# A decode-attention kernel: short instruction streams by loops, chunks of 64 keys, both output weights loaded last

## The chip, the cores and the metric

One core of one Trainium2 chip runs the whole program. The metric is device time in microseconds (us) of one execution. Unless a number is said to come from a profile it is the median of the timed runs; a profiled execution gives a span, which is some 2 us shorter than the time.

## The reference

Two independent attention blocks, A and B, each with its own weights and its own cache; the outputs are put side by side.

```python
B, Sq, D = 8, 1, 1024            # eight sequences, one new token each
H, Sk, Dh = 32, 4096, 128        # heads, cached keys, head size; all bf16
q = (x @ wq).reshape(B, Sq, H, Dh).transpose(0, 2, 1, 3)
scores = einsum("bhqd,bhkd->bhqk", q, k_cache) * Dh ** -0.5
o = einsum("bhqk,bhkd->bhqd", softmax(scores), v_cache)
out = o.transpose(0, 2, 1, 3).reshape(B, Sq, H * Dh) @ wo
```

Nothing of the caches is used twice. K and V of both blocks are 1073.7 MB, the four weights 33.6 MB, and all of it has to come from memory once.

## The kernel before

A tile is eight heads of one sequence: 128 partitions, each with 256 keys of 128 numbers, 64 KB a partition, 8.39 MB. There are 64 tiles of K and 64 of V. Three ring slots of that size hold what is loaded: two for K in turn, one for V.

VectorE multiplies a K tile by q chunk by chunk and folds it once; TensorE adds up the rest with identity matmuls; VectorE finishes the sum. After the whole tile: maximum, exponential (ACT), a masked copy `PM` of the probabilities (VectorE), and `PV` (TensorE), one tile behind.

```python
    CT = 32                                   # keys in a chunk
    NR = T // CT                              # 8 chunks a tile
    ...
        def make_mul(s):                      # VectorE, in place in the ring
            opMul[s] = add("dve", lambda e: e.tensor_tensor(
                v, v, qbc[:, n % 2, :].unsqueeze(1).to_broadcast([128, CT, Dh]), ALU.mult), [opT[("k", n, r)], opQbc[n]])
        def make_fold(s):                     # VectorE: 128 numbers to 64
        def make_eacc(s, fold):               # TensorE: 64 to 16, four identity matmuls a chunk
        def make_red(s):                      # VectorE: 16 to 1, two chunks later
    ...
        pv_at = {(n + 1, 5): n for n in range(NQ - 1)}   # PV after chunks 5 and 6 (counted from 0) of the next tile
```

The order of loads, and who frees a slot (cut):

```python
        put("wq", 0, 1); put("k", 0); put("wq", 1, 2)
        for n in range(NQ - 1):
            early = ...                                    # a K tile in two halves around wo
            put("k", n + 1, cuts=((0, NR // 2), (NR // 2, NR)) if early else None)
            put("v", n, 2)
            for c in range(NC):
                if n == done_at(c, NC, HB, B) + 1:         # n = 32 and n = 56
                    put("wo", c)                           # takes a K slot in the middle of the stream
                    late[n + 2] = c
        put("v", NQ - 1, cuts=...)                         # the last V in pieces
        put("wo_last", 0, 2)                               # the last 8 heads of B's wo
        plan.append(("v", NQ - 1, ((3 * NR // 4, 7 * NR // 8), (7 * NR // 8, NR))))
    ...
                    # B's wo: head h, row p to partition p: pieces of 2 KB
                    opT[(kind, n)] = dma(to[:, 0:cols].rearrange("p (h n) -> p h n", n=D),
                                         caches[-1][4][heads.start * Dh:heads.stop * Dh, :].rearrange("(h p) n -> p h n", p=128), key, [dep])
```

Everything is issued from straight lines of code: each engine's 64 tiles are written out, with every wait a constant.

## Time and profile before

| before | |
|---|---|
| time, median of 3 (range) | 2583.62 us (2583.49 to 2583.98) |
| profiled span | 2580.7 us |
| DMA | 1107.3 MB, 430 GB/s in the mean |
| VectorE busy | 2221.8 us, 86% |
| TensorE busy | 1219.7 us, 47% |
| one K and one V tile | 38.90 us |

From the page of the kernel before. `DMA` is the busy share in tenths in 40 equal slices, `GB/s` what moved in each; then the DMA queues with packets, MB and share of the time of all 16 DMA engines; then three groups of instructions (busy us, mean ns of one, and the idle time before them with its cause):

```profile
DMA  9999999999999999999999999999999999999998
GB/s 422 437 426 435 435 431 431 436 429 435 433 430 435 434 430 426 435 435 433 428 430 427 435 430 434 436 426 435 434 430 428 432 436 428 429 411 434 427 429 369
...
q1 hardware_dynamic: 23920, 1107.32, 99.5%
q8 instruction: 60, 0.98, 0.2%
q14 instruction: 18, 0.15, 0.0%
...
L305 DVE TENSOR_TENSOR ring<-ring,qbc 128x4096 bf16<-128x4096 bf16 x512 | 1169.0, 2283 | 327.0 <-DMA ring<-in_A_k_cache_dram 164.3
...
L310 DVE TENSOR_TENSOR ring<-ring 128x2048 bf16<-128x2048 bf16 x512 | 618.2, 1207 | 0.1
...
L327 DVE TENSOR_REDUCE s_sb<-red 128x32 f32<-128x512 f32 x512 | 348.3, 680 | 1.4 <-PE red L319 1.4
```

The DMA engines are busy throughout. VectorE idles before its multiply, 327 us in all, and what ends that idle time is a landing of K. Queue q1 holds the kernel's own loads. q8 and q14 hold instructions that the engines fetch: 78 packets, 1.13 MB, 0.2% of the time.

The timeline, one period of the steady state (start, duration, engine, line, operation; in brackets the idle time before it and its cause):

```profile
1015.35 2.29 DVE L305 TENSOR_TENSOR ring<-ring,qbc 128x4096 bf16<-128x4096 bf16 x1 [3.95 <-DMA ring<-in_A_k_cache_dram]
...
1046.41 0.33 SPq L158 DMA_DIRECT2D ring<-in_A_v_cache_dram  x1
...
1052.04 0.33 SPq L158 DMA_DIRECT2D ring<-in_A_k_cache_dram  x1
...
1054.25 2.29 DVE L305 TENSOR_TENSOR ring<-ring,qbc 128x4096 bf16<-128x4096 bf16 x1 [4.18 <-DMA ring<-in_A_k_cache_dram]
```

K lands at 1015.35 and at 1054.25: 38.90 us for 16.78 MB. The V load is issued 31.06 us into the tile, when PV has read the slot.

The chain of work that ended last, at the end of the kernel (start, duration, what):

```profile
2560.59 14.06 DMA ring<-in_B_v_cache_dram
...
2574.70 0.65 PE pv L359 x8
...
2575.37 0.61 ACT accS L367
...
2576.02 0.28 PE o L384 x4
...
2576.39 0.45 DVE on_sb L420
...
2576.88 1.08 PE proj L439 x32
...
2577.98 0.42 DVE orow L447
```

After the last piece of V lands at 2574.7, six short steps and the output follow, 6.0 us to the end of the span.

At the start, the second load of V and the load of K issued after it:

```profile
112.20 0.33 SPq L158 DMA_DIRECT2D ring<-in_A_v_cache_dram  x1
118.00 0.33 SPq L158 DMA_DIRECT2D ring<-in_A_k_cache_dram  x1
```

And the 40 us around B's `wo` (in the order of the columns: PE, PEld, DVE, ACT and POOL busy with counts, the clock, the DMA share, GB/s):

```profile
2290.00:2330.00 40.00, 18.23 (x196) 7.19 (x196) 21.50 (x18) 0.88 (x2) 0.00 (x0) 0.67 0.97 387
```

### The profile page before, as it was taken

To read this page: it belongs to the slowest core of one execution; us is meant where nothing else is said; L and a number is where in the kernel's file an instruction comes from. 1 tells how busy PE (TensorE), PEld (TensorE's weight loads), DVE (VectorE), ACT (ScalarE), POOL (GpSimd) and SP (SyncE) were. 2 spreads that over 40 slices of the span, in tenths; PEclk is the share of its full clock that TensorE was granted. 3 is DMA by queue.
4 is the path that set the end of the run, shared out by engine and by line. 5 is a ranking of instruction groups with operands and counts; after the bars stand their busy time and mean duration, and the time that the engine had idled before them with its cause. 6 is when DMAs were issued, how large, how long until landed. Compare 5 with 4: busy or idle time off the path is not lost.

```text
span 2580.7 us, 17905 instructions
## 1 busy us (share of the span) xinstructions
PE 1219.7 (47%) x7768; PEld 374.6 (15%) x7768; DVE 2221.8 (86%) x1809; ACT 105.2 (4%) x273; POOL 5.7 (0%) x23
## 2 busy tenths in 40 slices
PE   2454454453554454454553445445345445453445
PEld 0111111111111111111111111111112111110112
DVE  3898898898898898898895889889889889887897
ACT  1100000000000000000000000000000000000000
POOL 0000000000000000000000000000000000000000
PEclk7665655655656655656655566565565565565656
DMA  9999999999999999999999999999999999999998
GB/s 422 437 426 435 435 431 431 436 429 435 433 430 435 434 430 426 435 435 433 428 430 427 435 430 434 436 426 435 434 430 428 432 436 428 429 411 434 427 429 369
DMA packets 24094, 1108.50 MB, mean 430 GB/s; under 512 B 2304, under 2 KB 2368, under 8 KB 6480
## 3 DMA queue, kind: packets, MB, share of 16 engines
q1 hardware_dynamic: 23920, 1107.32, 99.5%
q8 instruction: 60, 0.98, 0.2%
q14 instruction: 18, 0.15, 0.0%
q10 hardware_dynamic: 96, 0.05, 0.0%
HBM read 1107.33 MB, written 0.03 MB: 429 GB/s over the span
## 4 chain that ended last, share of the span: by engine, by line
DMA 51%; DVE 46%; PE 2%; issue 1%; SPq 0%; ACT 0%; DVEq 0%
DMA ring<-in_A_k_cache_dram 26%; DMA ring<-in_B_k_cache_dram 24%; DVE ring L305 24%; DVE ring L310 12%; DVE s_sb L327 6%; DVE PM L347 3%; PE red L319 2%; DVE rmax L333 1%; DMA ring<-in_B_v_cache_dram 1%; DVE rtmp L335 0%; DVE ngm L338 0%; PE pv L359 0%; SPq L158 0%; DVE rl L407 0%; DVE on_sb L414 0%
## 5 line engine op out<-in xcount | busy, mean ns | idle before, releaser
L319 PE MATMUL red<-ring,ident 128*128 128x512 bf16 x2048 | 836.5, 554 | 1321.2 <-DVE ring L310 1320.9
L305 DVE TENSOR_TENSOR ring<-ring,qbc 128x4096 bf16<-128x4096 bf16 x512 | 1169.0, 2283 | 327.0 <-DMA ring<-in_A_k_cache_dram 164.3
L310 DVE TENSOR_TENSOR ring<-ring 128x2048 bf16<-128x2048 bf16 x512 | 618.2, 1207 | 0.1
L319 PEld LDWEIGHTS red<-ring,ident 128*128 128x128 bf16 x2048 | 202.4, 120 | 1859.4 <-DVE ring L310 1590.8
L327 DVE TENSOR_REDUCE s_sb<-red 128x32 f32<-128x512 f32 x512 | 348.3, 680 | 1.4 <-PE red L319 1.4
L359 PE MATMUL pv<-ring,PM 128*32 128x512 bf16 x4096 | 320.2, 468 | 1.3 <-DMA ring<-in_B_v_cache_dram 1.3
L347 DVE TENSOR_TENSOR PM<-pe,own_h 128x2048 bf16<-128x2048 bf16 x64 | 146.2, 2284 | 0.7 <-ACT pe L341 0.7
L359 PEld LDWEIGHTS pv<-ring,PM 128*32 128x32 bf16 x4096 | 113.2, 113 | 216.1 <-issue 164.3
L341 ACT ACTIVATE pe<-s_sb,ngm 128x256 bf16<-128x256 f32 x64 | 32.5, 508 | 1008.0 <-DVE ngm L338 1008.0
L367 ACT ACTIVATE accS<-pv 128x512 bf16<-128x512 f32 x64 | 38.2, 597 | 846.0 <-PE pv L359 846.0
L295 ACT ACTIVATE qbc<-misc 128x128 bf16<-128x128 f32 x64 | 17.8, 278 | 580.6 <-PE misc L290 580.6
L333 DVE TENSOR_REDUCE rmax<-s_sb 128x1 f32<-128x256 f32 x64 | 26.9, 420 | 2.2
L290 PE MATMUL misc<-q_sb,selb 8*32 8x128 bf16 x512 | 26.2, 295 | 1.5 <-ACT q_sb L278 1.5
L377 PE MATMUL o<-accS,E 128*32 128x32 bf16 x512 | 18.1, 177 | 0.0
L335 DVE TENSOR_SCALAR rtmp<-half,rmax 128x32 f32<-128x32 f32 x64 | 15.4, 241 | 2.2
L290 PEld LDWEIGHTS misc<-q_sb,selb 8*32 8x32 bf16 x512 | 9.2, 103 | 54.7 <-issue 54.7
L377 PEld LDWEIGHTS o<-accS,E 128*32 128x32 bf16 x512 | 14.8, 94 | 13.6 <-ACT accS L367 8.1
L439 PE MATMUL proj<-ring,on_sb 128*8 128x256 bf16 x256 | 12.1, 372 | 9.4 <-DMA ring<-in_A_wo_dram 5.8
L338 DVE TRANSPOSE_TENSOR_REDUCE ngm<-rtmp 128x1 f32<-128x32 f32 x64 | 13.5, 211 | 2.2
L399 PEld LDWEIGHTS o<-rsum,own_m 128*128 128x128 f32 x64 | 14.5, 333 | 4.4 <-ACT pe L341 3.3
L399 PE MATMUL o<-rsum,own_m 128*128 128x8 f32 x64 | 13.8, 355 | 2.4 <-ACT pe L341 2.4
L269 PE MATMUL o<-ring,xT 128*8 128x512 bf16 x64 | 6.8, 599 | 11.0 <-DMA ring<-in_A_wq_dram 11.0
(36 smaller groups left out, 71.2 us busy)
## 6 DMA issues: line engine op xcount, KB each, us to landing
ring<-in_B_k_cache_dram SPq DMA_DIRECT2D x6, 4096.0 KB, 36.0
ring<-in_B_wo_dram SPq DMA_DIRECT2D x1, 6144.0 KB, 36.9
ring<-in_B_v_cache_dram SPq DMA_DIRECT2D x1, 4096.0 KB, 31.8
ring<-in_B_v_cache_dram SPq DMA_DIRECT2D x1, 2048.0 KB, 36.4
ring<-in_B_wo_dram SPq DMA_DIRECT2D x1, 2048.0 KB, 13.9
ring<-in_B_v_cache_dram SPq DMA_DIRECT2D x2, 1024.0 KB, 15.0
ring<-in_A_k_cache_dram SPq DMA_DIRECT2D x32, 41.6
ring<-in_A_v_cache_dram SPq DMA_DIRECT2D x32, 27.5
```

The costliest lines, as they stand in the source:

```text
L290: x = e.matmul(misc[32 * g:32 * (g + 1), 0:Dh], selb[rows, b, i, :], q_sb[rows, c, j * Dh:(j + 1) * Dh], start=(i == 0), stop=(i == 1), ti ...
L305: opMul[s] = add("dve", lambda e: e.tensor_tensor(v, v, qbc[:, n % 2, :].unsqueeze(1).to_broadcast([128, CT, Dh]), ALU.mult), [opT[("k", n ...
L310: return add("dve", lambda e: e.tensor_tensor(v[:, :, 0:64], v[:, :, 0:64], v[:, :, 64:128], ALU.add), [opMul[s]])
L319: i = e.matmul(dst, ident[:], v[:, :, j, :], start=(j == 0), stop=(j == 3))
L327: opRed[s] = add("dve", lambda e: e.tensor_reduce(s_sb[:, n % 2, r * CT:(r + 1) * CT], red_ps[s % 4][:, :].rearrange("p (t w) -> p t w", w ...
L333: opRmax[n] = add("dve", lambda e: e.tensor_reduce(rmax[:], s_sb[:, n % 2, :], AX.X, ALU.max), [opRed[NR * n + NR - 1]])
L341: opExp[n] = add("act", lambda e: e.activation(pe[:], s_sb[:, n % 2, :], ACTF.Exp, bias=ngm[:, n % 2:n % 2 + 1], scale=scale, accum_out=rs ...
L347: opPM[n] = add("dve", lambda e: e.tensor_tensor(PM[:], pe[:].unsqueeze(2).to_broadcast([128, T, HQ]), own_h[:].unsqueeze(1).to_broadcast( ...
L359: i = e.matmul(pv_ps[32 * q:32 * (q + 1), :], PM[:, t:t + 4, :].rearrange("p t j -> p (t j)"), v[:, t * Dh:(t + 4) * Dh], start=(g == 0), ...
L367: opAcc[n] = add("act", lambda e: e.activation(accS[:], pv_ps[:], ACTF.Copy), [opPV[n], _at(opExt, n - 1)])
L377: x = e.matmul(o_ps[MB * hb:MB * (hb + 1), H * b:H * (b + 1)], E[:, i, PH - 1 - u:PH - 1 - u + MB], accS[:, i * 128 + H * u:i * 128 + H * ...
L399: x = e.matmul(o_ps[:, HQ * B * HB + B * (HQ * hb + j):HQ * B * HB + B * (HQ * hb + j + 1)], own_m[:, j, 0:1].to_broadcast([128, 128]), rs ...
```

## The change

Its intent: a shorter tail and fewer breaks in the stream of loads (both `wo` after all of K and V, in long rows, B's in three pieces of 24, 6 and 2 heads); fewer VectorE instructions (chunks of 64 keys, four a tile); one broadcast matmul for q in place of eight; and a program in which tiles 3 to 62 are a loop of two tiles on TensorE and on VectorE, with wait values that grow in registers.

The core of the diff, cut:

```diff
-    CT = 32
+    CT = 64
@@ the loop: only PE and DVE, tiles 3 to 62, two tiles in the body
+        straight(0, at[0])
+        with eng.Fori(0, rounds) as i:
+            grown = {s: eng.snap(i * s) for s in sorted(set(step.values()))}
+            for j in range(size):
+                for key, val in waits[at[0] + j]:
+                    eng.wait_ge(sems[key], grown[step[key]] + val)
+                emit(ops[at[0] + j])
+        straight(at[-1], len(ops))
+LOOPS = {"pe": True, "dve": True}
@@ the loads
+        plan = [("wq", 0, 1), ("k", 0, 0), ("wq", 1, 2)]
+        for n in range(NQ - 1):
+            plan.append(("k", n + 1, (n + 1) % 2))
+            plan.append(("v", n, 2))
+        plan += [("v", NQ - 1, NQ % 2), ("wo", 0, 2), ("wo", 1, (NQ - 1) % 2)]
+        wo_cuts = ((0, H - 8), (H - 8, H - 2), (H - 2, H))
@@ q: transposed once, then one matmul a tile
+                op = add("pe", emit, [...])                   # 8 transposes, for each of 4 head blocks
+                opQT[c] = opQT["last"] = add("dve", ... tensor_copy(qT[...], misc_bf16[...]), [op])
+            opQb[n] = add("pe", lambda e: e.matmul(misc[:, 0:Dh], qst[:, n % 2, :], ident[:], start=True, stop=True), [...])
@@ the order
+                if n == 0 and r == 1:
+                    for c in range(1, NC):
+                        make_q(c)
+                        make_qT(c)                            # B's, in tile 0
+                if r == 2 and n >= 1:
+                    make_pv(n - 1, 0, RG // 2)
+                if r == 3 and n >= 1:
+                    make_pv(n - 1, RG // 2, RG)
```

## The prediction

> **What bounds the kernel now.** The DMA. The page's slices show it at 9 tenths in 39 of 40, mean 430 GB/s; the queue table gives 1107.3 MB. In the steady state (timeline, 1000 to 1080 us) a tile of K plus a tile of V, 16.78 MB, takes 38.9 us between K landings: 431 GB/s. The Trainium skill, "DMA: Bandwidth & Descriptors", Specifications, puts the fabric's ceiling at 435 GB/s; the trace agrees that little is left. VectorE is busy about 34.8 us a tile, then waits some 4 us for K. The bytes do not change, so a large gain is impossible.
>
> **Where DMA could fall idle.** V has one ring slot, so V's load is issued when PV ends, 31.1 us after the tile's first multiply (1015.35 to 1046.41). Issue to landing takes 26.4 us at least, against 21.9 us for the first load into an empty queue: V is issued about 4.5 us before DMA would idle. K is issued far earlier (41.5 us to landing).
>
> **What the change does.**
> 1. Chunks of 64. Multiply, fold and reduce now follow at 2.21, 1.13 and 0.60 us, about 0.07 us of each fixed. Twelve instructions fewer: 34.8 to about 34 us a tile, off the critical path. PV's second half now follows the third fold: that ends at about 26.5 us, then eight matmuls (2.1 to 3.6 us) and 32 of PV (1.9 to 3.5 us): 30.5 to 33.5 us, where DMA would idle at 35.5. No stall.
> 2. q by one matmul: seven small matmuls a tile fewer, two small ACT copies more, nothing on the path.
> 3. The loop: [...] The Trainium skill, "Runtime: NRT & Kernel Launch", Instruction fetch mechanics, says a taken branch whose target isn't in the fetch window stalls; at a tile's boundary VectorE waits for K anyway. Instruction traffic (60 packets, 0.98 MB) should mostly vanish: about 2 us of DMA.
> 4. wo last. B's wo now comes in rows of 2 KB, and slowly (387 GB/s in 2290 to 2330 us): about 4 us gained by long rows. At the end, the last V piece landed at 2574.7 and the span ended at 2580.7. The last piece is now two heads of wo: 8 matmuls, copy, output, about 3.6 us: 2.4 us gained.
> 5. Startup loses. B's q transposes put four VectorE copies after the second chunk of tile 0; they wait for B's wq (landing about 62.8 us), 64 matmuls and eight ACT copies. VectorE, free at 58 us, stalls to about 73; tile 1 starts near 89 instead of 82.2, and the second V load is issued at 120 to 122 instead of 112.2, after the queue ran dry at about 119. Cost: 3 to 4.5 us, once.
>
> **Sum.** -4 (wo rows) -2.4 (tail) -2 (instructions) +3.5 (startup): about -5 us. Predicted 2578 us, range 2568 to 2590. Faster by over 2%: 0.01; within 2%: 0.95; slower: 0.04.
>
> **What would show it.** Still 38.8 to 39 us a tile; VectorE busy down by about 50 us, its wait for K up; V issued 30.5 to 33.5 us into the tile; a VectorE wait of about 15 us near 58 us and a DMA dip near 120; no dip near 2300 us; last landing to end 3.6 us; far fewer instruction packets.
>
> **What would make it wrong.** Register waits or branches costing VectorE over 4 us a tile, or PV ending over 35 us into the tile: DMA would idle in every tile, 1% for each 0.4 us. Or instruction refetches at each branch adding DMA traffic.

## More of the kernel before

The built program of TensorE has 996 KB, that of VectorE 121 KB.

The built program of TensorE is now 151 KB, that of VectorE 11 KB.

## The result, and the profile after

| | before | after |
|---|---|---|
| time, median of 4 (range) | 2583.55 (2582.24 to 2583.98) | 2566.47 (2565.43 to 2568.11) |
| profiled span | 2580.7 | 2565.5 |
| VectorE busy | 2221.8 | 2170.7 |
| TensorE busy | 1219.7 | 1106.8 |
| one K and one V tile | 38.90 | 38.69 |
| V load issued, us into the tile | 31.06 | 30.09 |
| last landing to end of span | 6.0 | 3.3 |

The ratio is 0.9935 (95% interval 0.9921 to 0.9949). Ratios are the mean time of one kernel's fast runs over that of the other's of the same rounds, so not quite the ratio of the medians quoted. The gain is 17.1 us, or 0.7%. The prediction was 5 us, and its range ended 1.5 us above the measured time.

The page of the kernel after, the lines that answer to those shown of before:

```profile
GB/s 425 426 437 431 435 431 435 431 436 431 435 435 432 435 431 436 430 437 430 437 431 435 431 434 432 434 433 433 433 433 432 434 433 433 433 434 432 434 432 379
...
q1 hardware_dynamic: 19360, 1107.32, 99.8%
q8 instruction: 9, 0.15, 0.0%
...
q14 instruction: 5, 0.04, 0.0%
...
L316 DVE TENSOR_TENSOR ring<-ring,qbc 128x8192 bf16<-128x8192 bf16 x256 | 1132.0, 4422 | 305.5 <-DMA ring<-in_B_k_cache_dram 153.9
...
L321 DVE TENSOR_TENSOR ring<-ring 128x4096 bf16<-128x4096 bf16 x256 | 582.6, 2276 | 0.0
...
L339 DVE TENSOR_REDUCE s_sb<-red 128x64 f32<-128x1024 f32 x256 | 312.2, 1220 | 2.5 <-PE red L331 2.5
```

The same 1107.32 MB arrive, in larger packets. The GB/s no longer fall below 430 in any slice from the third to the last but one; before, twelve slices did. The instruction packets fell from 60 to 9 on q8 and from 18 to 5 on q14. VectorE's idle time before its multiply is still ended by K: DMA bounds this kernel as it did the other.

The clock granted to TensorE differs, 0.605 in the profile before and 0.689 in this one. It is not the cause: a_ct32 below ran at 0.601 and was as fast as after, a_unroll ran at 0.688 and was 9 us slower.

The steady state, from the timeline:

```profile
1012.52 4.42 DVE L316 TENSOR_TENSOR ring<-ring,qbc 128x8192 bf16<-128x8192 bf16 x1 [4.80 <-DMA ring<-in_A_k_cache_dram]
...
1042.61 0.33 SPq L198 DMA_DIRECT2D ring<-in_A_v_cache_dram  x1
...
1050.12 0.33 SPq L198 DMA_DIRECT2D ring<-in_A_k_cache_dram  x1
...
1051.21 4.43 DVE L316 TENSOR_TENSOR ring<-ring,qbc 128x8192 bf16<-128x8192 bf16 x1 [4.78 <-DMA ring<-in_A_k_cache_dram]
```

A period is 38.69 us. Two loads of 128 packets of 64 KB take, at 2.42 us a packet (the median in the trace) and 16 engines, 38.7 us: no loss shows in this period.

The end, from the chain of work:

```profile
2521.07 36.21 DMA ring<-in_B_wo_dram
...
2557.43 5.35 PE proj L415 x117
...
2562.80 0.42 DVE orow L419
```

The chain stands on the first piece of B's `wo`. The projection then runs for 5.35 us, while the smaller pieces land; the last one lands at 2562.2 by its semaphore events. From there to the end of the span are 3.3 us instead of 6.0.

The start, from the timelines of VectorE and of the load queue:

```profile
69.58 0.19 DVE L291 COPY qT<-misc 128x64 bf16<-128x64 bf16 x1 [11.88 <-PE misc L287]
...
71.83 4.42 DVE L316 TENSOR_TENSOR ring<-ring,qbc 128x8192 bf16<-128x8192 bf16 x1
...
87.16 4.42 DVE L316 TENSOR_TENSOR ring<-ring,qbc 128x8192 bf16<-128x8192 bf16 x1
```

```profile
117.25 0.33 SPq L198 DMA_DIRECT2D ring<-in_A_v_cache_dram  x1
124.76 0.33 SPq L198 DMA_DIRECT2D ring<-in_A_k_cache_dram  x1
```

VectorE does wait for B's q transposes (11.88 us for the first copy, and it was free from 57.7), and the second V load is issued 5 us later than before, as the prediction said; but at 117.25, not at 120 to 122.

### The profile page after: what moved, and what is told of

The parts are those of the page before. It is cut to its first block, busy times and chain, and to the rows that moved or that the text cites. A ratio compares the mean times of both kernels' runs of the same rounds, so it can differ in the third digit from the quotient of the medians.

```text
span 2565.5 us, 18370 instructions
## 1 busy us (share of the span) xinstructions
PE 1106.8 (43%) x7712; PEld 393.2 (15%) x7712; DVE 2170.7 (85%) x1043; ACT 129.9 (5%) x401; POOL 2.5 (0%) x14
## 3 DMA queue, kind: packets, MB, share of 16 engines
q1 hardware_dynamic: 19360, 1107.32, 99.8%
## 4 chain that ended last, share of the span: by engine, by line
DMA 51%; DVE 28%; issue 16%; PE 4%; another core or an unknown queue 0%; ACT 0%; DVEq 0%; SPq 0%
DMA ring<-in_B_k_cache_dram 25%; DMA ring<-in_A_k_cache_dram 25%; DVE ring L316 10%; DVE ring L321 10%; PE red L331 4%; DVE s_sb L339 4%; DVE PM L356 3%; DMA ring<-in_B_wo_dram 1%; DVE rmax L345 1%; DVE rtmp L346 0%; PE proj L415 0%; ACT PM L277 0%; PE o L271 0%; DVEq L121 0%
## 5 line engine op out<-in xcount | busy, mean ns | idle before, releaser
L316 DVE TENSOR_TENSOR ring<-ring,qbc 128x8192 bf16<-128x8192 bf16 x256 | 1132.0, 4422 | 305.5 <-DMA ring<-in_B_k_cache_dram 153.9
L331 PE MATMUL red<-ring,ident 128*128 128x512 bf16 x2048 | 775.6, 548 | 1396.5 <-DVE ring L321 1396.5
L321 DVE TENSOR_TENSOR ring<-ring 128x4096 bf16<-128x4096 bf16 x256 | 582.6, 2276 | 0.0
L331 PEld LDWEIGHTS red<-ring,ident 128*128 128x128 bf16 x2048 | 237.7, 127 | 1843.6 <-DVE ring L321 1498.7
L339 DVE TENSOR_REDUCE s_sb<-red 128x64 f32<-128x1024 f32 x256 | 312.2, 1220 | 2.5 <-PE red L331 2.5
L368 PE MATMUL pv<-ring,PM 128*32 128x512 bf16 x4096 | 269.5, 410 | 4.6 <-DVE PM L356 4.6
L386 PEld LDWEIGHTS o<-accS,E 128*32 128x32 bf16 x1024 | 31.4, 101 | 49.8 <-issue 48.6
L386 PE MATMUL o<-accS,E 128*32 128x32 bf16 x1024 | 38.1, 185 | 0.7 <-ACT accS L376 0.7
L391 ACT ACTIVATE o_sb<-o 32x32 f32<-32x32 f32 x64 | 11.8, 185 | 440.5 <-PE o L386 439.8
L415 PE MATMUL proj<-ring,on_sb 128*8 128x256 bf16 x256 | 11.1, 357 | 18.5 <-DMA ring<-in_A_wo_dram 9.6
L298 ACT ACTIVATE qst<-qT 128x128 bf16<-128x128 bf16 x64 | 18.7, 293 | 1.0 <-DVE qT L291 1.0
```

Of the source, the lines that this page charges most:

```text
L298: opSt[n] = add("act", lambda e: e.activation(qst[:, n % 2, :].rearrange("p (j m) -> p j m", m=MP), from_.unsqueeze(2).to_broadcast([128, ...
L316: opMul[s] = add("dve", lambda e: e.tensor_tensor(v, v, qbc[:, n % 2, :].unsqueeze(1).to_broadcast([128, CT, Dh]), ALU.mult), [opT[("k", n ...
L321: return add("dve", lambda e: e.tensor_tensor(v[:, :, 0:64], v[:, :, 0:64], v[:, :, 64:128], ALU.add), [opMul[s]])
L331: i = e.matmul(dst, ident[:], v[:, g, :, j, :], start=(j == 0), stop=(j == 3))
L339: opRed[s] = add("dve", lambda e: e.tensor_reduce(s_sb[:, n % 2, r * CT:(r + 1) * CT], red_ps[s % 2][:, :].rearrange("p (t w) -> p t w", w ...
L368: i = e.matmul(pv_ps[32 * q:32 * (q + 1), :], PM[:, t:t + 4, :].rearrange("p t j -> p (t j)"), v[:, t * Dh:(t + 4) * Dh], start=(g == 0), ...
```

## The experiments

Each ran in five rounds against the kernel before (b_nowo has four results). Times without a label are of kernels named here; "after" is 2566.47 (first call) and 2566.01 (control in the third call). The calls ran on different chips; the kernel before took 2583.00 to 2583.55 us in them, so a comparison across calls is good to about half a microsecond. The traces kept of a_unroll, b_pv4 and b_longrows are of another execution than the times of single instructions quoted of them.

The theories. T1: instruction packets hold up single DMA engines, and a load has landed only when the slowest of 16 engines has done its share. T2: the gain comes from issuing V 1 us earlier. T3: the gain comes from moving `wo` out of the stream. T4 (added later): the unrolled code costs time in the compute engines, not in DMA. "Rings" in the quoted texts are the queues of the 16 DMA engines.

### 1. Loops undone: a_unroll

```diff
-LOOPS = {"pe": True, "dve": True}
+LOOPS = {"pe": False, "dve": False}
```

> After with both loops unrolled (same instructions on the engines, constant wait values). Theory T1 (instruction fetch): the packets of instruction fetch come back (about 60 instead of 9), each holds up one of the 16 DMA rings by about 0.5 us, the rings drift apart and those ahead run dry; the interior of the stream (groups of 8.39 MB at 19.35 us in after) loses 6 to 9 us, so about 2573 to 2576 us. Rival T2 (the gain comes from the V load being issued 1 us earlier in the tile, 30.1 instead of 31.1 us): unchanged within 1 us of after (2566). Rival T3 (wo in the middle of the stream disturbs it): unchanged too.

Measured: 2575.31 us (2575.17 to 2576.07), correct. That is 9 us slower than after, at the upper end of what T1 said. The queue lines of its page:

```profile
q8 instruction: 60, 0.98, 0.2%
q14 instruction: 13, 0.11, 0.0%
```

The rest is as in after: V is issued 30.1 us into the tile (1015.74 to 1045.83 in its timeline), the order of instructions is the same. T2 and T3 can't explain this half of the gain.

### 2. More time for V: b_pv4

```diff
-        pv_at = {(n + 1, 5): n for n in range(NQ - 1)}
+        pv_at = {(n + 1, 4): n for n in range(NQ - 1)}
```

> Before with PV one chunk earlier (after the fifth chunk instead of the sixth), so V is issued about 27 us into the tile instead of 31: 4 us more slack. T1 with drifting rings: more slack lets the rings drift further before one runs dry, so a part of the loss goes: 2 to 6 us faster than before, 2578 to 2582. T2: all of the interior loss goes, 7 us faster or more, 2576. T3: no change.

Measured: 2583.25 us beside 2583.15 of before, correct. V was issued about 27.3 us into the tile (1015.27 to 1042.59), 4 us earlier, and nothing came of it. T2 is out. So is the part of my T1 that had expected a gain here: more slack lets the leading engines run further ahead, but the time is that of the slowest one, which has no slack to use.

### 3. Long rows alone: b_longrows

```diff
-  dma(to[:, 0:cols].rearrange("p (h n) -> p h n", n=D), caches[-1][4][heads.start * Dh:heads.stop * Dh, :].rearrange("(h p) n -> p h n", p=128), ...)
+  dma(to[:, 0:cols], caches[-1][4].rearrange("(p r) n -> p (r n)", r=H)[:, heads.start * D:heads.stop * D], ...)
```

> Before with B's wo read in long contiguous rows (48 KB and 16 KB) in place of 2 KB rows; the result for B is wrong on purpose (rows of wo go to other partitions), the bytes are the same. The prediction's term for the rows: 4 us faster, 2579.5. From the packets alone (4096 of 0.088 us over 16 rings against 512 of 32 KB at 1.21 us): 22.6 against 19.4 us, 3.3 us faster, 2580.3. If the place of wo in the stream costs and not its rows (T3): no change.

Measured: 2582.04 us beside 2583.15, result wrong: 1.1 us, with ranges that overlap (2580.90 to 2583.18 and 2582.36 to 2583.92). The prediction's 4 us for the rows is not there. The load queue shows that the dip near 2300 us has another cause than the rows:

```profile
2278.30 0.33 SPq L158 DMA_DIRECT2D ring<-in_B_wo_dram  x1
2312.35 0.33 SPq L158 DMA_DIRECT2D ring<-in_B_k_cache_dram  x1
```

6.29 MB of `wo` are issued at 2278.30 and the next load 34 us later, because `wo` sits in a K slot. At 433 GB/s they take 14.5 us. DMA had 383 GB/s in 2290 to 2330 us with long rows too (387 before). Its busy share there was 0.90 with long rows and 0.97 before: most engines stood idle in the time that the short rows had taken. That may be a part of why the rows cost so little here; how large a part was not measured. (The "512 of 32 KB" is a slip; 256 such packets at 1.21 us give its 19.4 us.)

### 4. No `wo` in the stream: b_nowo

```diff
                 if n == done_at(c, NC, HB, B) + 1:
-                    put("wo", c)
-                    late[n + 2] = c
+                    pass
-                first = heads.start == 0 or HB == 1
+                first = True
```

(The cut of the K tiles beside them went too.)

> Before without the two loads of wo in the middle of the stream (A's 8.39 MB, B's first 6.29 MB) and their projections; wrong result on purpose. 14.68 MB at 19.35 us for 8.39 MB are 33.9 us, and the short rows 2.4 us more: 2546.9 if their place costs nothing. T3 (wo takes a K slot, and the queue runs dry behind it): 3 to 5 us less, 2542 to 2544.

Measured: 2547.89 us beside 2583.24, wrong result: 35.35 us less. The bytes alone are 33.9, and the short rows, at what experiment 3 measured for all of them, up to 1.1. About half a microsecond is left for the place. T3 falls as well, although the dip at 2300 us is plain to see in the profile. A dip in the mean of 16 engines is no loss of time if the slowest engine works through it; the others merely stop ahead of it. The kept trace of b_longrows shows such a moment: from 2312.0 to 2313.5 us one engine has a packet in hand and fifteen have none.

### 5. Short rows in the kernel after: a_wo2k

The same exchange in the other direction: B's `wo`, still last, in rows of 2 KB.

> After with B's wo read in rows of 2 KB as before read it, still last; B's result wrong on purpose. If rows of 2 KB cost what their packets take (0.088 us each, 4096 over 16 rings: 22.6 us instead of 19.4): 3 us slower than after, 2569.5. If the gain of item 4 came from the place in the stream alone: as after.

Measured: 2567.66 us (2567.00 to 2568.48), wrong result: 1.2 to 1.7 us slower than after's two medians, where the packets' durations gave 3. Together with experiment 3 the rows are worth 1 to 2 us. Why they cost less than their packets' durations say was not settled for this kernel, where `wo` is last.

### 6. Instructions that do nothing: a_fill, a_fill2, a_fill24

GpSimd is idle after the first 10 us. It was given a stream of instructions that touch nothing, released tile by tile:

```diff
+        def make_fill(n):
+            def emit(e):
+                for _ in range(240):
+                    i = e.drain()
+                return i
+            add("pool", emit, [opPM[n]])
```

A first form with NOPs (a_fill) did not run. Its expectation stood as follows.

> After, loops kept, with 240 NOPs a tile (15,360 in all, 0.98 MB of instructions) on the idle GpSimd, paced by the tile's PM. It adds instruction traffic and nothing else. T1: about 60 more instruction packets and 5 to 9 us more than after (2571 to 2575), spread over the stream. T2 and T3: as after, 2566, plus at most the 2.3 us that 0.98 MB take at 430 GB/s.

With drains:

> After with its loops kept, and 240 drain instructions a tile (about 15,000, 0.97 MB of instructions, as many bytes as the unrolled TensorE stream has) on the idle GpSimd, paced by the tile's PM. It adds instruction traffic and touches no engine or wait of the path. T1 (instruction fetch holds up DMA rings): about 60 more instruction packets and the unrolled kernel's loss, 6 to 9 us more than after: 2572 to 2576. Rival T4 (the unrolled kernel lost its 9 us in the engines, not in DMA): as after, 2566, plus at most the 2.3 us that 0.97 MB take at 430 GB/s.

Measured: 2646.00 us (2643.81 to 2647.69), correct. 80 us slower than after: T1's direction, but ten times its size. T4 can't explain it, since TensorE and VectorE run the looped code of after: VectorE is busy for 2170.7 us in both. From its page, and its steady state:

```profile
GB/s 428 426 431 432 430 423 429 414 423 419 426 416 427 412 418 424 416 429 413 424 418 422 419 426 416 413 428 413 414 429 412 415 427 414 423 420 423 419 426 341
...
q14 instruction: 123, 1.01, 0.1%
q8 instruction: 9, 0.15, 0.0%
```

```profile
1000.08 4.43 DVE L316 TENSOR_TENSOR ring<-ring,qbc 128x8192 bf16<-128x8192 bf16 x1 [6.11 <-DMA ring<-in_A_k_cache_dram]
...
1030.17 0.33 SPq L198 DMA_DIRECT2D ring<-in_A_v_cache_dram  x1
...
1037.68 0.33 SPq L198 DMA_DIRECT2D ring<-in_A_k_cache_dram  x1
...
1040.46 4.43 DVE L316 TENSOR_TENSOR ring<-ring,qbc 128x8192 bf16<-128x8192 bf16 x1 [6.47 <-DMA ring<-in_A_k_cache_dram]
```

The period went from 38.69 to 40.38 us here, with V issued at the same 30.09 us into the tile. Two packets of 8 KB a tile came on q14; by volume they are nothing, 1.01 MB in 2644 us.

What makes them dear is seen in the trace's records of single packets. Each load ends with a completion write by each of the 16 DMA engines, and the last of these is the landing. The table is worked out from the semaphore events of the kept traces: the first, the fifteenth and the last of the 16 writes of a load, as means over all loads that begin to land in 1000 to 1300 us. (a_peloop and a_dveloop, with one loop each, come in experiment 7.)

```
kernel      first to 15th   first to last (us)
before           4.6            5.1
after            1.8            3.5
a_unroll         5.3            5.7
b_pv4            6.1            6.6
a_fill2          1.5            8.6
a_peloop         1.5            5.9
a_dveloop        4.8            6.1
```

In a_fill2 fifteen engines finish a load within 1.5 us of each other and then wait for one, which is 7 us behind. So GpSimd's packets delay one engine, always the same one or nearly so. The records don't name the engine, but in this trace a load packet starts 3 to 4 ns before the end of the one before it on its engine, so the packets of one engine can be strung together as long as it has no pause. Around an instruction packet that engine's records show: the packet itself, 0.31 us in the median, in which it takes no load packet, and then a load packet that takes longer, mostly 2.77 us instead of 2.42. That sets the engine back by 0.5 to 0.9 us a packet, 0.65 in the median; over 122 of the 123 packets, all that could be placed so, it comes to 76 us. 80 us over 118 extra packets are 0.68 us apiece, which agrees.

The Trainium skill, "DMA: Bandwidth & Descriptors", Queues, rings and completion order, says that a DMA engine takes the queue rows for which it has work in turn, a packet at a time. The records agree: an instruction packet gets in between two load packets of one engine. The other fifteen did not take over that engine's share of the load: they finished and waited.

A smaller dose tests the slope:

> After with 24 drains a tile on GpSimd in place of 240: 97 KB of instructions, about 12 packets of 8 KB. The large filler cost 80 us for about 120 such packets, 0.65 us each: 12 x 0.65 = 8 us slower than after if the cost goes with the packets and they go to one ring; nothing if the drains themselves disturb only when they are many, 0.2 us by bytes.

Measured: 2570.87 us (2570.71 to 2572.21), correct: 4.9 us slower than the control (2566.01) for 12 packets more on q14 (17 instead of 5). It is less than the 8 us expected and twenty times what 97 KB take at 430 GB/s. That the first packets are cheaper fits with an engine which at first was not the last one, but this was only argued.

### 7. One loop at a time: a_peloop and a_dveloop

```diff
+LOOPS = {"pe": True, "dve": False}     # a_peloop
+LOOPS = {"pe": False, "dve": True}     # a_dveloop
```

> After unchanged, as the control for this chip: 2565 to 2568.

> After with TensorE's loop kept and VectorE unrolled (TensorE's program 151 KB, VectorE's 72 KB instead of 11). If TensorE's stream (the 16 KB packets, 60 against 9) made the 9 us: within 1 to 2 us of after. If VectorE's (8 KB packets, some 8 more, which may all go to one ring, at the 0.6 us apiece that the GpSimd filler showed): 5 us slower than after.

> After with VectorE's loop kept and TensorE unrolled (program of 989 KB instead of 151). If TensorE's stream made the 9 us: 7 to 9 us slower than after, 2573 to 2575. If VectorE's did: 3 to 4 us slower only.

Measured, all correct:

| kernel | q8 | q14 | time (range) | to the control |
|---|---|---|---|---|
| after_again | 9 | 5 | 2566.01 (2565.03 to 2568.03) | |
| a_peloop | 9 | 13 | 2573.24 (2571.84 to 2575.34) | +7.2 |
| a_dveloop | 60 | 5 | 2575.81 (2575.20 to 2577.55) | +9.8 |
| a_unroll (other call) | 60 | 13 | 2575.31 (2575.17 to 2576.07) | +9.3 |

q8 carries TensorE's stream: 60 packets of 16 KB (983 KB) are its 989 KB, 9 (147 KB) are its 151 KB. q14 carries the others' in packets of 8 KB. Either stream alone costs nearly the whole 9 us, and both together cost no more. Costs of two streams that are spent on different DMA engines don't add: the slower one counts. In a_unroll nine of the 13 q14 packets lie on two strung-together engines that have no q8 packet at all. Neither expectation had that; "5 us" and "7 to 9 us" for the two alone were near, but I had taken them for rivals.

A q8 packet is dear too. In a_unroll its engine takes no load packet for 0.9 to 1.1 us, and the next one takes 0.5 us longer: about 1.55 us. If all 51 extra packets went to one engine, that would be 80 us; they cost 9, so they are spread. The traces show over how many: in before, one engine strung together from 2 to 2304 us carries the 1st, 9th, 17th, 25th, 33rd, 41st and 49th packet of q8, and another, to 2313 us, the 2nd, 10th and so on to the 50th; a_ct32_unroll has two such runs of seven. So these packets went to eight engines in turn, seven or eight each where after has one or two. Six or seven more at 1.55 us make 9.3 to 10.9 us, an estimate from these records; measured are 9.8 (a_dveloop) and 9.3 (a_unroll).

VectorE's packets of 8 KB set their engine back by more than GpSimd's: 0.97 us for most of the 13 in a_peloop (0.59 to 0.98), 11.3 us in all, where the five of after make 3.5. On one engine that would be 7.8 us more; measured are 7.2. The table in experiment 6 fits: in a_peloop one engine finishes 4.3 us behind the other fifteen, in a_dveloop several lag.

### 8. Chunks of 32 again: a_ct32 and a_ct32_unroll

```diff
-    CT = 64
+    CT = 32
```

with PV after chunks 5 and 6 as before, B's q after the fourth chunk; once with loops and once with `LOOPS` off.

> After with chunks of 32 keys as before, loops kept (VectorE's program 16 KB). If the size of the chunks matters only through the instruction stream: as after, 2565 to 2568. If the fixed cost of VectorE's twelve extra instructions a tile, or the later V load (about 31 us into the tile instead of 30.1), costs: slower by more than 1 us.

> After with chunks of 32 keys and no loops: VectorE's program 121 KB as in before, against 72 KB in the unrolled kernel with chunks of 64. Theory: the 8 KB packets all go to one ring at about 0.65 us each, and this ring is the slowest: 6 more packets, 3 to 4 us slower than the unrolled kernel (2575.3), 2578 to 2579.5, and with the rows (1.2) and the tail (2.5) the sum reaches before. If the slowest ring is one of TensorE's: as the unrolled kernel, 2575 to 2576, and 4 us of the gain stay unexplained.

Measured, both correct: 2566.84 us (2566.41 to 2567.74) and 2577.97 us (2577.48 to 2580.11). With loops, the size of the chunk is worth 0.4 to 0.8 us against after's two medians, within the noise. Without, chunks of 32 are 2.7 us slower than chunks of 64 (2575.31): VectorE's program is then 121 KB instead of 72 KB, and q14 has 19 packets instead of 13. The loops are worth 11.1 us at the old chunk size.

### 9. B's `wo` in one piece: a_onecut

```diff
-        wo_cuts = ((0, H - 8), (H - 8, H - 2), (H - 2, H))
+        wo_cuts = ((0, H),)
```

> After with B's wo as one load of 8.39 MB instead of pieces of 24, 6 and 2 heads. All 128 projection matmuls then follow the last landing (5.3 to 5.8 us in the trace of after) instead of the last few: 3 to 5 us slower than after, 2569.5 to 2571.5. If projection is hidden some other way: no change.

Measured: 2571.67 us (2571.04 to 2572.35), correct: 5.2 to 5.7 us slower than after. All 128 matmuls, 5.85 us in its timeline, follow the landing. The pieces do what they are meant to.

### 10. q transposes later: a_q2

```diff
-                if n == 0 and r == 1:
+                if n == 0 and r == 2:
                     for c in range(1, NC):
                         make_q(c)
                         make_qT(c)
```

> After with B's q projection and q transposes one chunk later (after the third chunk of tile 0 instead of the second), so that VectorE waits some 6 us for them instead of 14 and the second V load is issued near 112 us instead of 117.25. The trace of after shows 0.65 us of excess in the group of loads there: 0.6 us faster than after (2565.9), or the same if that excess is the ramp of the rings.

> The version with B's q transposes one chunk later, again on another chip: 2564.5 to 2565.5, 1 to 1.5 us faster than after, if its first result (2564.87) was not chance.

Measured: 2564.87 us (2564.53 to 2565.41), and on another chip 2565.38 us (2564.90 to 2566.01), correct. This is the fastest version, 0.6 to 1.6 us ahead of after's two medians; the ranges of single runs overlap, so its lead is likely rather than certain. The load queue shows that the mechanism works; the second V load is back at the time it had in before:

```profile
112.27 0.33 SPq L198 DMA_DIRECT2D ring<-in_A_v_cache_dram  x1
119.59 0.33 SPq L198 DMA_DIRECT2D ring<-in_A_k_cache_dram  x1
```

## Why the prediction was right or wrong

What held: DMA bounds both kernels. VectorE's busy time fell by 51 us (about 50 predicted), off the path. V is issued at 30.1 us (30.5 to 33.5 predicted), with no stall. The loop's register additions and branches cost nothing that shows. The tail gained 2.8 us by the profiles (2.4 predicted), and a_onecut confirms its mechanism. The VectorE wait near 58 us came, at its place.

What failed, in order of size:

1. "Instruction traffic (60 packets, 0.98 MB) should mostly vanish: about 2 us of DMA." This is the step that failed. The direction was right, the term was worth 9.3 us at chunks of 64 (a_unroll) and 11.1 us at chunks of 32 (a_ct32 against a_ct32_unroll). I divided bytes by the rate of all 16 DMA engines. A packet holds up one engine, by about 1.55 us if it has 16 KB and 0.5 to 1.0 us if it has 8 KB, and the load waits for the slowest of 16. TensorE's packets went to eight engines in turn, those of a_fill2 nearly all to one. a_fill2 shows it without any other change: 1 MB of instructions on one engine cost 80 us.
2. "Twelve instructions fewer ... off the critical path." True of VectorE's time, as a_ct32 shows. But I did not see that fewer instructions also means fewer packets: without loops the smaller chunks cost 2.7 us.
3. "-4 (wo rows)". Measured 1.1 (b_longrows) and 1.2 to 1.7 (a_wo2k). I read the drop to 387 GB/s near 2300 us as a cost of short rows. It was still there with long rows, and b_nowo shows that almost no time is lost by it.
4. "+3.5 (startup)". The mechanism was right, the sizes were each on the safe side: tile 1 began at 87.16 instead of 89 and V came 30.1 us into it, so the load was issued at 117.25. a_q2, which takes most of the stall away (2.7 us of waiting before the first copy instead of 11.9), gains about 1 us.

The sum, with measured terms: loops 11.1, chunks 0.4 to 0.8 on top, rows 1.2, tail 2.8, startup about -1, place of `wo` 0.5: about 15 of the 17 us. Some 2 us stay open; they lie between before and a_ct32_unroll, which share the chunk size and the straight code.

The three other terms of the forecast were right in sum by luck: -4, -2.4 and +3.5 make -2.9, and measured they make -3.0 (-1.2, -2.8 and about +1). The rows were put some 3 us too high, the startup some 2.5 us, with opposite signs.

## What to carry to other kernels

A kernel bound by DMA at 99% can still have time to gain in what the page gives as 0.2%: a load has landed when the slowest of its 16 engines is done, so every small packet counts with the time that it holds one engine, not with its share of the bytes. A loop whose body isn't fetched anew each round takes most of the fetches away (here 60 packets of TensorE became 9), and it was worth more than everything else in the change. Before a dip in the mean rate is called a loss, take away what seems to cause it and time the kernel.

## What the Trainium skill lacked or had wrong

- "Runtime: NRT & Kernel Launch", Instruction fetch mechanics: it calls run-time control flow expensive and says that kernels prefer full unrolling where possible. Here 30 rounds of a loop of two tiles were 9.3 us faster than the same code unrolled (11.1 us with chunks of 32). The fetched bytes on q8 are those of the program, 9 packets of 16 KB, so the loop's body was not fetched again. VectorE's busy time was 2170.7 us with and without the loop; no cost of a branch showed.
- The same section calls fetching at the block boundaries mostly hidden. It was not hidden from loads that fill the 16 DMA engines: 0.68 us for each 8 KB packet of GpSimd (118 packets, 80 us), and about 1.55 us of one engine's time for a 16 KB packet of TensorE.
- The same section gives refills in 16 KiB blocks. Here TensorE's packets have 16,384 bytes, those of the other engines' streams 8,192, and in a_fill2 many of these come singly, 7.8 us or more apart.
- "DMA: Bandwidth & Descriptors", Queues, rings and completion order: that an engine takes its queue rows in turn is borne out. The section names refill among the uses of row 14; the profile here has TensorE's stream on q8 and the others' on q14. No page says what a refill costs a load in flight, nor how a stream is dealt out: TensorE's went to eight engines in turn (before, a_ct32_unroll), and in a_fill2 one engine was 7 us behind the fifteen others.
